# A short piece moved to the end of every value product, and the last 512 queries of the last head group cut in two

## The chip, the cores and the metric

The kernel runs on one NeuronCore of a Trainium2 chip. The metric is the device time of one execution in microseconds; the figure quoted is the median over the runs. TensorE (PE) does the matmuls, VectorE (DVE), ScalarE (ACT) and GpSimd (POOL) the elementwise work, and SyncE (SP) issues most transfers.

## What is computed

One input x (2048 rows, 512 columns, bf16) goes through two branches, and a gate per row mixes them. Branch A is attention with 32 heads of 16 and a sliding window of 256; branch B is a gated feed-forward layer of width 1376.

```python
def _A_ref(x, wqkv, wo):
    H = 32; Dh = D // H; W = 256
    q, k, v = qkv[0], qkv[1], qkv[2]
    scores = jnp.einsum("bhqd,bhkd->bhqk", q, k) * (Dh ** -0.5)
    mask = (idx[:, None] - idx[None, :] >= 0) & (idx[:, None] - idx[None, :] < W)
    scores = jnp.where(mask[None, None], scores, -1e9)
    p = _softmax(scores, axis=-1)
    o = jnp.einsum("bhqk,bhkd->bhqd", p, v)
    return o.transpose(...).reshape(B, S, D) @ wo

def _B_ref(x, w1, w3, w2):
    return (silu(x @ w1) * (x @ w3)) @ w2

g = sigmoid((x * gate_w).sum(-1, keepdims=True))
return g * _A_ref(x, A_wqkv, A_wo) + (1 - g) * _B_ref(x, B_w1, B_w3, B_w2)
```

## The kernel before

**Tiling of the attention.** The 32 heads form 4 groups c of 8 heads, and the queries form 4 tiles t of 512. Keys are taken in blocks of 64 (HK). A *piece* (j, q0, q1, col) is key block j against queries q0 to q1, written at column col of a score buffer. A block of 64 keys is seen by at most 320 queries (64 + 256), which is the widest piece; the narrowest has 64 queries. `bursts(c, t)` (L271) packs the pieces of a tile into *bursts* of up to 512 columns: 4 bursts for t = 0, 5 for each other tile, 76 over all groups.

**One burst** (`add_burst`, L663): for each piece 4 score matmuls on TensorE (L684; keys 32 x 128 are the stationary operand, which holds two heads' worth of 64 keys in its columns), into the tile `big`, of which there is one (4 banks of PSUM). ScalarE takes the exponential of it into a tile `e` (L692). Then triangles are masked, one at the near and one at the far edge of the window, where a piece has such an edge: on GpSimd with two instructions each (L708), or on VectorE (L702) for the far edges of bursts 2 and 3.

**One value product** (`add_pv`, L729): for each entry of `ranges(c, t)` (L267; here the whole tile of 512 queries) it collects all pieces of the tile's bursts, clipped to the range, into the list `work`, and issues 8 matmuls for each piece (L758). The eight use eight different parts of the array (two row groups of 64, four column groups of 32), and take 64 keys x 32 value columns as stationary operand; one of the value columns is 1 and gives the sum for the softmax. They accumulate in two banks of the pool `g`. VectorE then transposes both banks (L768), takes the reciprocal (L777), multiplies (L778) and transposes back into `OT` (L783). A tile of queries 512 and up has 12 pieces of 320, 192, 320, 192, 320, 128, 64, 320, 128, 64, 256 and 256 queries in this order; a tile of the first 512 has 9: 320, 192, 320, 128, 64, 320, 192, 320, 64.

**The rest on TensorE** is full matmuls of 128 x 512: projections of q and k (L313) and v (L360), the up products of the feed-forward layer (L454; a last slice of 96 columns at L504), the down products (L552), and the output projection (L582). The last 128 rows are done in another order (`add_last`, L601): output projection (L611) first, then the down product in column ranges of 256, 128 and 128 (L636), each with its own output transfer.

**The order of the work.** Every piece of work is an `Op` with a duration, dependencies and buffers, and a list scheduler (L872 to L1002) simulates the engines and writes each engine's order at build time; on the chip every engine then runs its list in order, with semaphores. Bursts, value products and projections have due times: `when(c, n) = T0 + PACE * (19 c + n)` (L807), with T0 = 12.5 and PACE = 2.62 (L803). On TensorE a burst that is due goes first; a value product goes behind a burst, or once it has been ready for 2.6 us, or when no burst is left (L953); an item with a due time that has passed goes ahead of the feed-forward work, which fills the rest. The durations in the scheduler for a value product are 0.14 us plus its columns over 2400 (L792), plus 0.1 if no burst is ahead of it.

`LAST` (L265) names the last tile of the last group, (3, 3). Its vector work gets a rank of its own (L796).

Of the kernel before, what the change touches and what calls it, by code (L numbers as in the profile page):

```python
# [16 lines left out]
HK = 64  # L17
# [5 lines left out]
def kernel(  # L23
# [68 lines left out]
    def hold(pool, key, n):  # L92

        refs[(pool, key)] = n
# [127 lines left out]
    def bank(key, dtype=F32, shape=(P, 512)):  # L222
        n = slot("g", key)
        g_tile[key] = ps.tile(list(shape), dtype, name=f"g{n}")
        return g_tile[key]
# [39 lines left out]
    LAST = (NDC - 1, NTC - 1)  # L265

    def ranges(c, t):  # L267

        return [(512 * t, 512 * t + 512)]

    def bursts(c, t):  # L271

        b, q = 8 * t, 512 * t
        if t == 0:
            r = [[(0, 0, 320), (5, 320, 512)], [(1, 64, 384), (6, 384, 512), (4, 448, 512)],
                 [(2, 128, 448), (4, 256, 448)], [(3, 192, 512), (7, 448, 512)]]
        else:
            r = [[(0, 0, 320), (-2, 0, 192)], [(1, 64, 384), (5, 320, 512)],
                 [(2, 128, 448), (6, 384, 512), (-4, 0, 64)],
                 [(3, 192, 512), (-3, 0, 128), (7, 448, 512)], [(-1, 0, 256), (4, 256, 512)]]  # L280
        out = []
        for ps_ in r:
            col, o = 0, []
            for j, q0, q1 in ps_:
                o.append((b + j, q + q0, q + q1, col))
                col += q1 - q0
            out.append(o)
        return out
# [4 lines left out]
    def add_proj(c, t0, t1, is_q):  # L293
# [8 lines left out]
        if first:  # L302
            hold("qk", (c, t), len(bursts(c, t)) + (len(bursts(c, t + 1)) if t + 1 < NTC else 0))
# [359 lines left out]
    def add_burst(c, t, n):  # L663


        key = (c, t, n)
        pieces = bursts(c, t)[n]
        w = sum(q1 - q0 for _, q0, q1, _ in pieces)
        hold("big", key, 1)
        hold("e", key, sum(any(q0 < b and q1 > a for _, q0, q1, _ in pieces) for a, b in ranges(c, t)))  # L670
        deps = []
        for j, q0, q1, _ in pieces:
# [56 lines left out]
    def add_pv(c, t, qa, qb):  # L729


        keys = [("p", c, qa, i) for i in range(2)]
        for k in keys:
            hold("g", k, 1)
        st = {}
        nq = qb - qa
        used, work = [], []
        for n, pieces in enumerate(bursts(c, t)):
            for j, q0, q1, col in pieces:
                a, b = max(q0, qa), min(q1, qb)  # L740
                if a < b:
                    work.append(((c, t, n), j, a, b, col + a - q0))
                    if (c, t, n) not in used:
                        used.append((c, t, n))
        rel = [("e", k) for k in used]

        def v_of(j, i, w):
            lo = i * HK
            if j % 2 == i:
                return Vn[lo:lo + HK, j // 2, i * VW + w * (DH + 1):i * VW + w * (DH + 1) + 32]  # L750
            return Vs[lo:lo + HK, j // 2, w * (DH + 1):w * (DH + 1) + 32]

        def pe():
            st["pv"] = pv = [bank(k) for k in keys]
            for n, (k, j, a, b, col) in enumerate(work):
                for i in range(2):
                    for u in range(4):
                        nc.tensor.matmul(pv[i][32 * u:32 * u + 32, a - qa:b - qa],  # L758
                                         lhsT=v_of(j, i, 4 * c + u),
                                         rhs=e_tile[k][i * HK:i * HK + HK, u, col:col + b - a],  # L760
                                         start=(n == 0), stop=(n == len(work) - 1),
                                         skip_group_check=True)

        def turn(i):
            def f(eng):
                if i == 0:
                    st["t1"] = xp.tile([P, 2, 512], F32, name="xs23")
                nc.vector.transpose(out=st["t1"][:, i, 0:nq], in_=st["pv"][i][:, 0:nq])  # L768
            return f

        nb = nq // 32

        def norm(eng):
            rden = sb.tile([P, 2, 16, 1], F32, name="rden")
            st["on"] = on = sb.tile([P, 16, 2, DH], BF16, name="on")
            v = st["t1"][:, :, 0:nq].rearrange("p i (b r) -> p i b r", r=32)
            nc.vector.reciprocal(out=rden[:, :, 0:nb, :], in_=v[:, :, :, DH:DH + 1])  # L777
            nc.vector.tensor_tensor(out=on[:, 0:nb].rearrange("p b i d -> p i b d"),  # L778
                                    in0=v[:, :, :, 0:DH],
                                    in1=rden[:, :, 0:nb, :].to_broadcast([P, 2, nb, DH]), op=ALU.mult)  # L780

        def back(eng):
            nc.vector.transpose(out=OT[:, c * S + qa:c * S + qb],  # L783
                                in_=st["on"][:, 0:nb].rearrange("p b i d -> p (b i d)"))

        deps = [o for k in used for o in e_mask[k]]
        js = [j for _, j, _, _, _ in work]
        deps += [V_op[m] for m in range(min(js) // 2, max(js) // 2 + 1)]
        deps += [Vs_op[x] for x in range(min(js) // 8, max(js) // 8 + 1)]
        hold("t1", ("t1", c, qa), 1)  # L790
        cols = sum(b - a for _, _, a, b, _ in work)
        a = Op("PE", 0.14 + cols / 2400.0, pe, deps, acq=[("g", k) for k in keys], rel=rel, kind="pv")  # L792
        b0 = Op("DVE", 0.1 + nq * 0.0012, turn(0), [a], rel=[("g", keys[0])],
                acq=[("t1", ("t1", c, qa))], rank=-0.6)
        b1 = Op("DVE", 0.1 + nq * 0.0012, turn(1), [a, b0], rel=[("g", keys[1])], rank=-0.6)
        rk = -0.3 if (c, t) == LAST else 0.6  # L796
        n1 = Op("DVE", 0.5 + nq * 0.0011, norm, [b0, b1], rank=rk)
        o = Op("DVE", 0.15 + nq * 0.0011, back, [n1] + (z_op if c else []), rel=[("t1", ("t1", c, qa))], rank=rk)
        for m in range(qa // P, qb // P):
            pv_out[(c, m)] = o  # L800
        return a

    T0, PACE, NWARM = 12.5, 2.62, 6  # L803
    SEQ = [(t, n) for t in range(NTC) for n in range(len(bursts(0, t)))]
    per_c = len(SEQ)

# [30 lines left out]
    for c in range(NDC):  # L837
        for n, (t, k) in enumerate(SEQ):
            a = add_burst(c, t, k)
            a.need = when(c, n)  # L840
        for t in range(NTC):
            for qa, qb in ranges(c, t):
                a = add_pv(c, t, qa, qb)
                a.need = when(c, SEQ.index((t, 0)) + 5) + 1.0
# [40 lines left out]
    def ready_time(o, eng):  # L885
        r = 0.0
        for d in o.deps:
            lat = 0.0 if d.eng == eng else LAT.get((d.eng, eng), 0.08)
            r = max(r, d.end + d.lag + lat)
        return r  # L890
# [22 lines left out]
    while len(order) < len(ops):  # L913
# [3 lines left out]
        for e, lst in ready.items():  # L917
            cands = []
            for o in lst:
                if o.kind == "ffn" and not o.cont and o.seq != ffn_next:  # L920
                    continue
                r = max(ready_time(o, e), free_at[e])
                ok = True
                want = {}
                for pool, key in o.acq:
# [4 lines left out]
                    r = max(r, sorted(slots[pool])[n - 1][0] + 0.08)  # L930
# [8 lines left out]
            t = max(min(r for r, _ in cands), free_at[e])  # L939
# [25 lines left out]
            r, o = min(now, key=pkey)  # L965
# [7 lines left out]
        t, e, o = best  # L973
# [72 lines left out]
```

The softmax here doesn't subtract the row's maximum and nothing guards it: scores larger than these inputs give would overflow.

## Time and profile before

| | |
|---|---|
| median of 4 runs | 231.54 us (231.15 to 232.07) |
| the profiled execution | 232.07 us, span 230.2 us |
| TensorE clock granted | 1.00 of full speed |
| TensorE busy | 221.9 us (96% of the span) |
| VectorE, ScalarE, GpSimd busy | 178.8, 177.5, 175.1 us |
| score matmuls (L684) | 720, of 188 to 305 ns each |
| value product matmuls (L758) | 1440, of 189 to 300 ns each |
| full matmuls of the up products (L454) | 302 recorded with 320 weight loads, 380 ns each |
| exponential of one burst (L692) | 1.88 us for 512 columns |
| one triangle instruction on GpSimd (L708) | 448 ns, 368 of them |

The span is the time from the first to the last instruction in the profile. In a timeline, a row has its start, its length (us), engine, line, operation, what it writes and reads, its shape, how often it is repeated, and in brackets the idle time of the engine ahead of it and what ended it. PE is TensorE's matmuls, PEld its weight loads, which run beside the matmuls. Matmuls are pipelined, so the length of one (380 ns) is longer than the distance between two starts.

### The profile page before, as it was taken

The page shows a single profiled execution, that of the slowest core. Times are in us where ns is not written, and L with a number is a line of the kernel's source. Part 1 is how long each engine was busy: PE and PEld are TensorE (multiplying, and loading weights), DVE is VectorE, ACT ScalarE, POOL GpSimd, SP SyncE. Part 2 cuts the span into 40 slices and gives each one's busy share as a digit, 9 for nine tenths or more (in the row PEclk, how much of TensorE's full clock was granted, in tenths as well). Part 3 has the DMA queues.
Part 4 walks back from the last instruction along what each step waited for, and adds up shares of the span by engine and source line. Part 5 has one row for each costly group of instructions (what it writes and reads, how often), then busy time and mean ns, then how long its engine had stood idle before and what let it go on. Part 6 is the DMA issues. An engine that isn't in the chain of part 4 may idle for free.

```text
span 230.2 us, 7237 instructions
## 1 busy us (share of the span) xinstructions
PE 221.9 (96%) x3026; PEld 102.2 (44%) x3060; DVE 178.8 (78%) x312; ACT 177.5 (77%) x148; POOL 175.1 (76%) x395
## 2 busy tenths in 40 slices
PE   7999999999999999999999999999999999999995
PEld 4543344535434443535453435443443445354544
DVE  1467789999999999768758593959987688876754
ACT  3579899889888899796989799987899877977030
POOL 8049888989988888888778887877888878778200
PEclk9999999999999999999999999999999999999999
DMA  6999999400200000000000000000000000220202
GB/s 185 219 274 341 156 277 362 106 0 4 48 3 3 3 0 0 4 3 4 0 3 0 3 3 0 3 3 4 1 3 0 3 4 25 81 83 0 94 3 93
DMA packets 19697, 13.81 MB, mean 60 GB/s; under 512 B 8656, under 2 KB 19376, under 8 KB 19664
## 3 DMA queue, kind: packets, MB, share of 16 engines
q1 hardware_dynamic: 18560, 11.93, 19.6%
q0 software_dynamic: 432, 1.25, 3.3%
q8 instruction: 24, 0.39, 0.7%
q10 hardware_dynamic: 672, 0.16, 0.3%
q14 instruction: 9, 0.07, 0.1%
HBM read 8.55 MB, written 2.10 MB: 46 GB/s over the span
## 4 chain that ended last, share of the span: by engine, by line
PE 84%; DVE 8%; DMA 3%; issue 2%; ACT 1%; SPq 1%; ACTq 0%
PE g L454 27%; PE g L552 16%; PE big L684 10%; PE g L313 10%; PE g L758 8%; PE g L582 6%; PE g L360 4%; DMA e<-in_A_wqkv_dram 3%; PE g L504 2%; DVE hT L462 2%; PE g L636 1%; DVE kt L328 1%; DVE Vn L370 1%; ACT e L692 1%; DVE h L435 1%
## 5 line engine op out<-in xcount | busy, mean ns | idle before, releaser
L708 POOL TENSOR_SCALAR_AFFINE_SELECT e<-e 64x256 bf16<-64x256 bf16 x368 | 164.7, 448 | 32.1 <-ACT e L692 11.4
L692 ACT ACTIVATE e<-big 128x2048 bf16<-128x2048 f32 (+1 forms) x76 | 141.0, 1855 | 29.3 <-PE big L684 27.7
L454 PE MATMUL g<-xT,w_sb 128*128 128x512 bf16 x302 | 76.3, 380 | 1.4 <-issue 1.0
L454 PEld LDWEIGHTS <-w_sb 128*128 128x128 bf16 x320 | 29.1, 98 | 35.2 <-issue 4.0
L552 PE MATMUL g<-w_sb,hT 128*128 128x512 bf16 (+1 forms) x159 | 38.9, 380 | 1.3 <-issue 1.3
L768 DVE STREAM_TRANSPOSE xs<-g 128x512 f32<-128x512 f32 x32 | 21.9, 701 | 17.8 <-PE g L758 17.8
L435 DVE SCALAR_TENSOR_TENSOR h<-tt,g 128x512 bf16<-128x512 bf16 (+1 forms) x44 | 29.8, 677 | 5.0 <-ACT tt L430 4.6
L462 DVE TENSOR_TENSOR hT<-h,g 128x512 bf16<-128x512 bf16 x40 | 26.9, 674 | 4.8 <-PE g L454 4.3
L684 PE MATMUL big<-qt,kt 32*128 32x64 bf16 (+3 forms) x720 | 30.0, 254 | 0.4 <-ACT e L692 0.2
L430 ACT ACTIVATE tt<-g 128x512 bf16<-128x512 f32 (+1 forms) x44 | 26.1, 594 | 1.2 <-PE g L454 0.5
L684 PEld LDWEIGHTS <-kt 32*128 32x128 bf16 x720 | 12.0, 92 | 32.8 <-issue 31.1
L552 PEld LDWEIGHTS <-hT 128*128 128x128 bf16 (+1 forms) x165 | 15.0, 98 | 17.8 <-issue 1.4
L328 DVE TENSOR_TENSOR kt<-g,maskEO 128x1024 bf16<-128x1024 f32 (+1 forms) x17 | 19.6, 1151 | 3.0 <-PE g L313 2.9
L758 PE MATMUL g<-e,Vs 64*32 64x64 bf16 (+3 forms) x720 | 20.0, 253 | 0.0
L758 PE MATMUL g<-e,Vn 64*32 64x64 bf16 (+3 forms) x720 | 19.9, 254 | 0.0
L313 PE MATMUL g<-xT,wq_sb 128*128 128x512 bf16 (+1 forms) x66 | 17.9, 368 | 0.4 <-issue 0.3
L313 PE MATMUL g<-xT,wk_sb 128*128 128x512 bf16 (+1 forms) x64 | 17.0, 375 | 0.4 <-issue 0.2
L758 PEld LDWEIGHTS <-Vn 64*32 64x32 bf16 x720 | 15.1, 91 | 3.4 <-issue 1.1
L360 PE MATMUL g<-e,xT 128*128 128x512 bf16 x61 | 15.5, 380 | 0.4 <-DMA e<-in_A_wqkv_dram 0.2
L758 PEld LDWEIGHTS <-Vs 64*32 64x32 bf16 x720 | 15.2, 91 | 0.2
L702 DVE TENSOR_TENSOR e<-e,keep 128x512 bf16<-128x512 bf16 (+1 forms) x32 | 14.0, 442 | 0.6 <-ACT e L692 0.5
L582 PE MATMUL g<-xs,OT 128*128 128x512 bf16 x59 | 14.1, 380 | 0.1
(61 smaller groups left out, 153.7 us busy)
## 6 DMA issues: line engine op xcount, KB each, us to landing
w_sb<-in_B_w_dram SPq DMA_DIRECT2D x2, 864.0 KB, 7.7
w_sb<-in_B_w_dram SPq DMA_DIRECT2D x1, 1280.0 KB, 10.0
out_dram<-ot SPq DMA_DIRECT2D x19, 64.0 KB, 1.6
Vs<-Vn POOLq DMA_DIRECT2D x8, 136.0 KB, 3.6
w_sb<-in_B_w_dram SPq DMA_DIRECT2D x2, 512.0 KB, 4.8
OT<-in_A_x_dram SPq DMA_DIRECT2D x1, 1024.0 KB, 10.8
out_dram<-ot SPq DMA_DIRECT2D x6, 128.0 KB, 1.8
xs<-in_A_x_dram SPq DMA_DIRECT2D x2, 256.0 KB, 3.2
```

The costliest lines, as they stand in the source:

```text
L313: nc.tensor.matmul(b[:, 0:n], lhsT=(wq_sb if is_q else wk_sb)[:, dc, c * P:(c + 1) * P], rhs=xT[:, dc, t0:t1], start=(dc == 0), stop=(dc = ...
L360: nc.tensor.matmul(b[:], lhsT=xT[:, c, m * P:(m + 1) * P], rhs=wv_sb[:, c, :], start=(c == 0), stop=(c == NDC - 1))
L430: nc.scalar.activation(out=tl["tt"][0:m, :], in_=g_tile[key][0:m, :], func=ACT.Tanh, scale=0.5)
L435: nc.vector.scalar_tensor_tensor(out=tl["h1"][0:m, :], in0=tl["tt"][0:m, :], scalar=1.0, in1=g_tile[key][0:m, :], op0=ALU.add, op1=ALU.mult)
L454: nc.tensor.matmul(b[:], lhsT=wsb[:, dc, f * P:(f + 1) * P], rhs=xT[:, dc, t * 512:(t + 1) * 512], start=(dc == 0), stop=(dc == NDC - 1))
L462: nc.vector.tensor_tensor(out=h_of(t)[:, f, :], in0=tl["h1"][:], in1=g_tile[ku][:], op=ALU.mult)
L552: nc.tensor.matmul(b[:], lhsT=h_tile[t][0:fs, f, (m % 4) * P:(m % 4 + 1) * P], rhs=w2_sb[0:fs, f, :], start=(f == 0), stop=(f == NFC - 1))
L582: nc.tensor.matmul(b[:, 0:n], lhsT=OT[:, c * S + m * P:c * S + (m + 1) * P], rhs=wo_t[c // 2][:, c % 2, n0:n1], start=(c == 0), stop=(c == ...
L684: nc.tensor.matmul(big[:, u, col:col + q1 - q0], lhsT=kt[32 * u:32 * u + 32, (j % 8) * P:(j % 8 + 1) * P], rhs=qt[32 * u:32 * u + 32, q0 - ...
L692: nc.scalar.activation(out=e[:, :, 0:w], in_=tl["big"][:, :, 0:w], func=ACT.Exp, scale=SCALE)
L708: nc.gpsimd.affine_select(out=tri, in_=tri, pattern=[[0, 4], [-1 if far else 1, HK]], compare_op=ALU.is_ge, fill=0.0, base=-1 if far else ...
L758: nc.tensor.matmul(pv[i][32 * u:32 * u + 32, a - qa:b - qa], lhsT=v_of(j, i, 4 * c + u), rhs=e_tile[k][i * HK:i * HK + HK, u, col:col + b ...
```

## The change

Three things change, and a number. `ranges` returns two ranges of 256 queries for the last tile of the last group, so that `add_pv` makes two value products there. `bursts` packs the pieces of that tile in another way, cut at 256 queries, into five bursts of 512 columns: 16 pieces in place of 12. In `add_pv`, where there is more than one piece, the first piece of exactly 64 queries is taken out of the list and put at its end, in every value product; the matmuls that open and close the accumulation are by position. T0 becomes 12.0.

For a tile of queries 512 and up the order of pieces becomes 320, 192, 320, 192, 320, 128, 320, 128, 64, 256, 256, 64; for the first 512: 320, 192, 320, 128, 320, 192, 320, 64, 64. Each half of the last tile has 256, 256, 192, 192, 128, 128, 64, 64 (second half: 256, 256, 192, 192, 128, 128, 64, 64 with other keys).

```diff
     def ranges(c, t):
 
-        return [(512 * t, 512 * t + 512)]
+        q = 512 * t
+        return [(q, q + 256), (q + 256, q + 512)] if (c, t) == LAST else [(q, q + 512)]
 
     def bursts(c, t):
...
+        elif (c, t) == LAST:
+            r = [[(0, 0, 256), (-1, 0, 256)], [(1, 64, 256), (-2, 0, 192), (2, 128, 256)],
+                 [(-3, 0, 128), (-4, 0, 64), (3, 192, 256), (4, 256, 512)],
+                 [(3, 256, 512), (5, 320, 512), (0, 256, 320)],
+                 [(2, 256, 448), (1, 256, 384), (6, 384, 512), (7, 448, 512)]]
         else:
             r = [[(0, 0, 320), (-2, 0, 192)], [(1, 64, 384), (5, 320, 512)],
...
                     if (c, t, n) not in used:
                         used.append((c, t, n))
+        short = [x for x in work if x[3] - x[2] == HK]
+        if len(work) > 1 and short:
+            work.remove(short[0])
+            work.append(short[0])
         rel = [("e", k) for k in used]
...
-    T0, PACE, NWARM = 12.5, 2.62, 6
+    T0, PACE, NWARM = 12.0, 2.62, 6
```

## The prediction

> **What bounds the kernel now.** I read the page first, then the timeline of TensorE, then the timeline around the end.
>
> ```profile
> span 230.2 us, 7237 instructions
> PE 221.9 (96%) x3026; PEld 102.2 (44%) x3060; DVE 178.8 (78%) x312; ACT 177.5 (77%) x148; POOL 175.1 (76%) x395
> PE 84%; DVE 8%; DMA 3%; issue 2%; ACT 1%; SPq 1%; ACTq 0%
> ```
>
> The page says that TensorE is the bound: 96% busy, and 84% of the chain that ended last. A busy share hides what a matmul really costs, so I took the distance from the first weight load of one kind of work to the first weight load of the next. Three kinds alternate on TensorE: full matmuls (128x512), score bursts (L684) and value products (L758). Next, the timeline of a value product of queries 512 and up, with the burst ahead of it and the full matmuls behind it.
>
> ```profile
> 202.60 0.40 PE L684 MATMUL big<-qt,kt 32*128 32x320 bf16 x8
> ...
> 202.93 0.10 PEld L758 LDWEIGHTS <-Vn 64*32 64x32 bf16 x4 [0.21 <-issue]
> ...
> 203.57 0.20 PE L758 MATMUL g<-e,Vn 64*32 64x64 bf16 x4
> ...
> 203.61 0.32 PE L758 MATMUL g<-e,Vn 64*32 64x320 bf16 x4
> ...
> 203.98 0.29 PE L758 MATMUL g<-e,Vs 64*32 64x256 bf16 x4
> ...
> 204.21 0.76 PEld L454 LDWEIGHTS <-w_sb 128*128 128x128 bf16 x5
> ```
>
> The product takes 204.21 - 202.93 = 1.28 us for 12 pieces of 8 matmuls. The eight run side by side, so its pieces stream 2560 columns. A column costs 0.42 ns: the 16 matmuls of 512 columns at 211.80 take 3.62 us with a last one of 0.38, so (3.62 - 0.38) / 15 = 0.216 us each. That makes 2560 columns 1.08 us, and 0.20 us is lost. The same for a product of the first 512 queries, whose last piece has 64 columns and not 256:
>
> ```profile
> 129.41 0.32 PE L758 MATMUL g<-e,Vn 64*32 64x320 bf16 x4
> ...
> 130.22 0.21 PE L758 MATMUL g<-e,Vn 64*32 64x64 bf16 x4
> 130.36 0.11 PEld L552 LDWEIGHTS <-hT 128*128 128x128 bf16 x2
> ```
>
> It takes 0.95 to 0.96 us for 9 pieces with 1920 columns, that is 0.81 us, and loses 0.15. After the first groups of its last piece the next kind starts 0.15 us later; with 256 columns at the end it is 0.23 us. All 16 products of the trace repeat these two figures within 0.01 us (12 of 1.28, 4 of 0.96).
>
> TensorE's stretches of full matmuls add up too: 10 matmuls between two bursts take 2.27 us, which is 2.16 + 0.11 for the change of kind, and a burst takes 0.33 (202.60 to 202.93). From 8.34 us, when the weights of the value projection have landed, to the last matmul I find one stretch that is longer than this count, by 0.28 us:
>
> ```profile
> 32.04 1.88 ACT L692 ACTIVATE e<-big 128x2048 bf16<-128x2048 f32 x1 [0.19 <-PE big L684]
> ...
> 33.68 0.09 PEld L684 LDWEIGHTS <-kt 32*128 32x128 bf16 x1 [0.42 <-issue]
> ...
> 33.96 0.40 PE L684 MATMUL big<-qt,kt 32*128 32x256 bf16 x8 [0.21 <-ACT e L692]
> ```
>
> Here a burst had its weights at 33.68 but the one score buffer was still read by the exponential, which ended at 33.92. So the time is the sum of TensorE's work, plus 8.3 us ahead of it and 2.7 us behind it. The gaps of 0.16 us that the page puts down to issue are mostly matmuls missing from the records: the weight loads there are complete.
>
> **The change, part by part.** (1) *The short piece goes last* in the 11 whole products of queries 512 and up (12 less the split one). Same 96 matmuls and loads each. What it can save is the loss at the end: 0.20 against 0.15 us, since the product would end as those of the first 512 queries do. The start times say why: behind the sequence of a 128 and a 64 piece the loads no longer run ahead, the last two pieces of 256 start their eight matmuls spread over about 0.06 us, and the 256 columns stream after that. I take 0.045 us each, 11 x 0.045 = -0.50. Bounds: nothing is gained if the product is set by its number of matmuls (12 x 8 x 13.3 ns = 1.28 fits as well), and a last piece that is issued late loses 0.03 each; at best 0.06 each. So -0.66 to +0.33. In the four products of the first 512 queries a 64 piece goes behind another 64 piece: 4 x 0.01 = -0.04.
>
> (2) *The last product is split* into two halves of 256 queries. Each has 8 pieces (256, 256, 192, 192, 128, 128, 64, 64) with 1280 columns: 0.54 us and, as it ends on a 64, 0.15 lost: 0.69. Two are 1.38 in place of 1.28: **+0.10**. By the count of matmuls it would be 2 x 64 x 13.3 ns = 1.71, +0.43; that is the upper end, and +0.05 the lower (both halves losing 0.12). One more product may stand alone between full matmuls: +0.11 or nothing, I take +0.05, as the bursts of the last queries are still running when the first half is ready.
>
> The Trainium skill speaks against more and smaller matmuls: the page TensorEngine Tiling (Array Packing), section Instruction Overhead, gives every matmul about 60 cycles whatever its width. The rows differ: eight 64 column matmuls cost 0.04 us (203.57 to 203.61), 5 ns each, since they lie on eight tiles. By the page the 32 added matmuls would be 32 x 25 ns at its 2.4 GHz, an estimate of +0.8 us, and the whole change about +0.4 instead of what follows.
>
> (3) *Five bursts of the last queries are cut otherwise.* Each still has 512 columns (0.33 us), but 16 matmuls and loads more in all. A 64 piece between others streams 0.03 us and may wait for the next load. Bounds 0 (a burst of 2 and of 3 pieces both take 0.33) and +0.13 (two such places, each with the 92 ns of a load at L684 less 27). I take +0.05.
>
> (4) *Masks and VectorE.* GpSimd's triangles stay 12, but the last burst has 4 in place of 2. VectorE gets a second chain of transposes, reciprocal, product and transpose, of half the width; this is at most the 3.2 us of a whole one. All of it costs nothing if TensorE has other work meanwhile. The timeline of the end:
>
> ```profile
> 210.59 0.40 PE L684 MATMUL big<-qt,kt 32*128 32x256 bf16 x8
> ...
> 211.12 1.88 ACT L692 ACTIVATE e<-big 128x2048 bf16<-128x2048 f32 x1 [0.74 <-POOL e L708]
> ...
> 213.07 1.80 POOL L708 TENSOR_SCALAR_AFFINE_SELECT e<-e 64x256 bf16<-64x256 bf16 x4 [0.53 <-ACT e L692]
> ...
> 216.21 0.32 PE L758 MATMUL g<-e,Vn 64*32 64x320 bf16 x4
> ...
> 220.03 0.71 DVE L783 STREAM_TRANSPOSE OT<-on 128x512 bf16<-128x512 bf16 x1
> ...
> 221.40 1.03 PE L611 MATMUL g<-xs,OT 128*128 128x512 bf16 x4
> ```
>
> The chain behind the product ends at 220.74, 0.66 us before TensorE asks for it. With four triangles (3.6 us) and a last burst 0.5 us earlier the second half is ready near 216.2; even at 217.5 it ends at 218.2, and a chain of 3.2 us at 221.4. Work that does not need it lasts longer: from the last burst TensorE has 16.5 + 0.5 us, of which the projections of the last 256 queries and the last down products (0.86 + 0.86 + 2.45) depend on it, so the rest reaches to about 223. Slack 1.8 us. Without that cover each us of lateness would be a us of time. Transfers: no DMA is added, and output rows leave as before.
>
> (5) *T0 from 12.5 to 12.0* moves the due times of all bursts, products and projections 0.5 us ahead of the feed-forward work. It adds no work, and TensorE is full from 8.34 on, so there is nothing to win but the 0.28 us at 33.68. It can lose where a burst comes before its buffer is free, or where VectorE is full:
>
> ```profile
> 40.00:60.00 20.00, 19.49 (x327) 9.33 (x332) 19.61 (x38) 16.94 (x14) 17.90 (x37) 1.00 0.18 44
> ```
>
> In this row of the stretches VectorE (the third pair) is busy 19.61 of 20 us, and evacuates most of what TensorE writes. I take 0, with -0.28 to +0.6.
>
> **Sum:** -0.50 - 0.04 + 0.10 + 0.05 + 0.05 + 0 = -0.34 us. The profiled execution took 232.07 with a span of 230.2, so its span would be 229.9. It is 0.53 above the median of 231.54; on the median the forecast is **231.2 us**.
>
> **Rivals.** *A, clearly faster.* The ends add: -0.66 - 0.04 + 0.05 + 0 + 0 - 0.28 = -0.93 at the very most; with most of these, 230.75. For it: the one stall is due to the order, which changes. Against: nearly all must come true, as no other idle time exists.
>
> *B, the moved piece does nothing,* because a product is set by its number of matmuls. Then 0 + 0.43 + 0.11 + 0.05 = +0.59: 232.1. For it: 1.28 / 96 and 0.96 / 72 are both 13.3 ns. Against: starts inside a product follow the widths (0.13 us behind 320 columns, 0.04 behind 64), not the count.
>
> *C, slower:* the earlier bursts meet the full VectorE between 40 and 64 us. A burst's share of VectorE work there (a mask of 0.4, a fifth of a 3.2 us chain and of two evacuations of 1.8 together) is 1.2 to 1.4 us; if it runs ahead of the evacuations that free TensorE's buffers, TensorE stands still for about that long: -0.34 + 1.3 = +1.0, 232.5. It decides from a wait of 1.03 us on, below that the gain covers it. For it: the chain of waits runs through VectorE there without a gap. Against: eight gate reductions of about 0.8 us stand in the same stretch and can wait.
>
> **How the numbers follow.** A measurement of this kernel can tell about 0.3% (0.7 us) from no change: below 230.85 is faster, above 232.23 slower. Forecast 0.45 and B 0.06 lie between; A 0.27; C 0.22. So faster 0.27, same 0.51, slower 0.22. The range goes to A and C: 230.6 to 232.6; the forecast's own is 230.9 to 231.6.
>
> **What would show it.** Right: products of queries 512 and up last 1.23 us from first load to the next kind's load, halves 0.69, stretches of full matmuls keep 0.11 + 0.216 each, and the last matmul ends near 227.1. Products still at 1.28 and halves at 0.85 show B. A stretch of full matmuls or a burst more than 0.1 us over its count, with VectorE ahead of it, shows C; the same with the exponential ahead shows that the stall at 33.68 moved or grew. Wrong altogether would be an idle TensorE ahead of the last output projections.

## The result, and the profile after

The changed kernel takes 232.10 us (median of 47 runs), the kernel before 231.58 us (72 runs). The ratio is **1.0023, with a 95% interval of 1.0018 to 1.0028**: slower by half a microsecond, where a third of one less was forecast. The change is below the bound of 0.3% of the prediction, yet well outside the interval, and its sign is wrong. The measured 232.10 lies inside the wide range that the prediction's rivals had set (230.6 to 232.6) and outside the forecast's own (230.9 to 231.6).

The page of the changed kernel, the lines that answer to those shown of before:

```profile
span 230.2 us, 7347 instructions
PE 221.5 (96%) x3074; PEld 102.9 (45%) x3108; DVE 175.9 (76%) x310; ACT 180.2 (78%) x155; POOL 174.0 (76%) x395
PE 88%; DVE 4%; issue 3%; DMA 2%; ACT 1%; SPq 1%; DVEq 0%; ACTq 0%
```

The two spans are equal to 0.1 us, so the pages alone hide the loss. The profiled executions (231.87 and 232.07 us) lie on opposite sides of their medians, and the reason is at the start: the weights of the value projection had landed for a first matmul at 7.56 us after the change, at 8.34 before. I therefore measure from the first matmul of the value projection to the end of the last matmul, where TensorE has no pause of more than 0.06 us but the named ones: 8.34 to 227.45 = **219.11 us before, 7.56 to 227.38 = 219.82 after: +0.71**. This distance, always of the one profiled execution, is given for experiments below.

A whole product of queries 512 and up in the changed kernel, in the timeline (start, length, engine, line; lines are 6 to 10 higher than before, the value matmul is L768):

```profile
142.48 0.10 PEld L768 LDWEIGHTS <-Vn 64*32 64x32 bf16 x4
...
143.32 0.20 PE L768 MATMUL g<-e,Vn 64*32 64x64 bf16 x4
143.34 0.28 PE L768 MATMUL g<-e,Vs 64*32 64x256 bf16 x4
...
143.56 0.22 PE L768 MATMUL g<-e,Vn 64*32 64x64 bf16 x4
143.59 0.21 PE L768 MATMUL g<-e,Vs 64*32 64x64 bf16 x4
143.74 0.10 PEld L319 LDWEIGHTS <-wk_sb 128*128 128x128 bf16 x1
```

It takes 143.74 - 142.48 = 1.26 us (1.257 in the trace's nanoseconds), not 1.28 and not the forecast 1.23. The product does end 0.15 us behind the start of its second row group's last matmuls (143.59), as said. But its last eight matmuls still start over 60 ns (143.56 and on), not over the 35 ns of a product of the first 512 queries before the change. In nanoseconds from the first load, the last matmul starts at 1139, where before it started at 1081; it then streams 192 columns fewer (81 ns), which leaves a gain of 23 ns.

The first half of the split product:

```profile
211.01 0.26 PEld L690 LDWEIGHTS <-kt 32*128 32x128 bf16 x16 [0.43 <-issue]
...
211.35 0.10 PEld L588 LDWEIGHTS <-OT 128*128 128x128 bf16 x1
...
211.67 0.10 PEld L768 LDWEIGHTS <-Vn 64*32 64x32 bf16 x4 [0.23 <-issue]
...
212.21 0.27 PE L768 MATMUL g<-e,Vn 64*32 64x64 bf16 x8
...
212.44 0.55 PEld L588 LDWEIGHTS <-OT 128*128 128x128 bf16 x4
```

It takes 0.77 us (212.44 - 211.67), so two halves are 1.54 in place of 1.28. And between the burst (0.34 us with its 16 loads) and the product there is a stretch of one single full matmul (211.35 to 211.67, 0.32 us = 0.216 + 0.11). That is a change of kind which did not exist before.

There are more of those. Counted over the whole trace, full matmuls stand in 81 stretches, against 77 before. One is the half's, another is a single matmul ahead of a product at 79.64, and two stand behind a group of the tiled up products (L510) at 29.86 and here:

```profile
157.01 0.55 PEld L510 LDWEIGHTS <-w_sb 128*32 128x32 bf16 x16 [0.42 <-issue]
157.99 0.11 PEld L460 LDWEIGHTS <-w_sb 128*128 128x128 bf16 x2 [0.42 <-issue]
158.53 0.25 PEld L690 LDWEIGHTS <-kt 32*128 32x128 bf16 x12 [0.42 <-issue]
```

Two full matmuls between tiled ones and a burst take 0.54 us: 0.43 of work, 0.11 for the change. Last come the waits. The 0.28 us at 33.7 us is gone, and another has come near it:

```profile
33.34 1.23 DVE L334 TENSOR_TENSOR kt<-g,maskEO 128x1024 bf16<-128x1024 f32 x1
33.37 0.76 PEld L460 LDWEIGHTS <-w_sb 128*128 128x128 bf16 x5 [0.21 <-issue]
33.37 1.04 PE L460 MATMUL g<-xT,w_sb 128*128 128x512 bf16 x4
...
34.62 1.02 PE L460 MATMUL g<-xT,w_sb 128*128 128x512 bf16 x4 [0.21 <-DVE kt L334]
```

TensorE's up product waits until VectorE has read the keys out of a `g` buffer, which it finishes at 34.57: 0.37 us over the count for that stretch. And one product, at 90.26 us, stands still in the middle:

```profile
91.12 0.28 PE L768 MATMUL g<-e,Vs 64*32 64x256 bf16 x4
91.13 0.31 PEld L768 LDWEIGHTS <-Vn 64*32 64x32 bf16 x8
91.33 0.30 PE L768 MATMUL g<-e,Vn 64*32 64x256 bf16 x8
```

Its piece of 256 has started for one row group and waits 0.2 us for the other. GpSimd masks that burst meanwhile. The third of its five triangle instructions in this row ends at 91.28, and TensorE goes on 0.05 us later, at 91.33:

```profile
89.93 2.28 POOL L714 TENSOR_SCALAR_AFFINE_SELECT e<-e 64x256 bf16<-64x256 bf16 x5
```

The ledger, from the trace:

| part | us |
|---|---|
| ten products at 1.257, three at 0.948 | -0.25 |
| two halves in place of a whole | +0.26 |
| four more changes of kind, 0.11 each | +0.44 |
| wait at 33 us: 0.37 in place of 0.28 | +0.09 |
| product at 90.26 (1.423) and at 79.96 (1.005) against 1.280 and 0.958 | +0.19 |
| sum, against 0.71 measured in these two executions | +0.73 |

The product at 79.96 loses its 0.05 us at its start: one row group starts at once, the other at 80.03, which is 0.06 behind the end of a triangle instruction (79.97). This fits the same wait for a mask.

### The profile page after: what moved, and what is told of

It is laid out like the page before. It is cut to its first block, busy times and chain, and to the rows that moved or that the text cites. A ratio compares the mean times of both kernels' runs of the same rounds, so it can differ in the third digit from the quotient of the medians.

```text
span 230.2 us, 7347 instructions
## 1 busy us (share of the span) xinstructions
PE 221.5 (96%) x3074; PEld 102.9 (45%) x3108; DVE 175.9 (76%) x310; ACT 180.2 (78%) x155; POOL 174.0 (76%) x395
## 4 chain that ended last, share of the span: by engine, by line
PE 88%; DVE 4%; issue 3%; DMA 2%; ACT 1%; SPq 1%; DVEq 0%; ACTq 0%
PE g L460 29%; PE g L558 16%; PE g L319 11%; PE big L690 10%; PE g L768 8%; PE g L366 6%; PE g L588 6%; DMA e<-in_A_wqkv_dram 2%; PE g L510 1%; PE g L642 1%; DVE h L441 1%; DVE hT L518 1%; DVE xs L778 1%; DVE kt L334 1%; ACT tt L436 1%
## 5 line engine op out<-in xcount | busy, mean ns | idle before, releaser
L460 PEld LDWEIGHTS <-w_sb 128*128 128x128 bf16 x320 | 28.5, 98 | 35.7 <-issue 5.7
L778 DVE STREAM_TRANSPOSE xs<-g 128x512 f32<-128x512 f32 (+1 forms) x34 | 21.9, 669 | 16.9 <-PE g L768 16.7
L690 PE MATMUL big<-qt,kt 32*128 32x64 bf16 (+4 forms) x736 | 30.1, 252 | 0.3
L768 PE MATMUL g<-e,Vs 64*32 64x320 bf16 (+4 forms) x736 | 20.2, 251 | 0.0
L768 PE MATMUL g<-e,Vn 64*32 64x320 bf16 (+4 forms) x736 | 20.0, 252 | 0.0
L768 PEld LDWEIGHTS <-Vn 64*32 64x32 bf16 x736 | 15.6, 91 | 3.3 <-issue 1.9
L319 PE MATMUL g<-xT,wq_sb 128*128 128x512 bf16 (+1 forms) x66 | 16.7, 367 | 0.3 <-issue 0.3
L768 PEld LDWEIGHTS <-Vs 64*32 64x32 bf16 x736 | 15.6, 92 | 0.3
L366 PE MATMUL g<-e,xT 128*128 128x512 bf16 x61 | 14.8, 379 | 0.6 <-DMA e<-in_A_wqkv_dram 0.2
```

The lines of the kernel that those rows point to most:

```text
L319: nc.tensor.matmul(b[:, 0:n], lhsT=(wq_sb if is_q else wk_sb)[:, dc, c * P:(c + 1) * P], rhs=xT[:, dc, t0:t1], start=(dc == 0), stop=(dc = ...
L366: nc.tensor.matmul(b[:], lhsT=xT[:, c, m * P:(m + 1) * P], rhs=wv_sb[:, c, :], start=(c == 0), stop=(c == NDC - 1))
L460: nc.tensor.matmul(b[:], lhsT=wsb[:, dc, f * P:(f + 1) * P], rhs=xT[:, dc, t * 512:(t + 1) * 512], start=(dc == 0), stop=(dc == NDC - 1))
L690: nc.tensor.matmul(big[:, u, col:col + q1 - q0], lhsT=kt[32 * u:32 * u + 32, (j % 8) * P:(j % 8 + 1) * P], rhs=qt[32 * u:32 * u + 32, q0 - ...
L768: nc.tensor.matmul(pv[i][32 * u:32 * u + 32, a - qa:b - qa], lhsT=v_of(j, i, 4 * c + u), rhs=e_tile[k][i * HK:i * HK + HK, u, col:col + b ...
```

## The experiments

My theory after the result: the change is a sum of three independent parts, of which the moved piece gains, the split loses, and T0 = 12.0 loses because the scheduler makes another order of work out of it. Rivals stand with each run. All ratios are against the kernel before, run on the same chip.

**The moved piece alone.**

```diff
+        short = [x for x in work if x[3] - x[2] == HK]
+        if len(work) > 1 and short:
+            work.remove(short[0])
+            work.append(short[0])
```

> Before, with the short piece moved to the end and nothing else (T0 12.5, last tile whole). The order of work on TensorE is that of before, 77 stretches of full matmuls. Theory (three parts that add up: a small gain from the moved piece, a loss from the split, a loss from the order that T0 = 12.0 makes): products of queries 512 and up 1.257 us as in the changed kernel, 948 ns for the first 512, so 12 x -0.022 + 4 x -0.010 = -0.30 us, ratio 0.9987. Rival (the moved piece itself is what costs, through VectorE's or the buffers' timing): no gain or a loss, ratio 1.000 or more.

Ratio 0.9986 (0.9978 to 0.9995), 231.26 us; twelve products of 1.256 to 1.258 and four of 0.947 to 0.948; 77 stretches; distance 218.87, that is -0.24. The theory holds, the rival falls: this part is a gain.

**The split alone.**

```diff
-        return [(512 * t, 512 * t + 512)]
+        return [(q, q + 256), (q + 256, q + 512)] if (c, t) == LAST else [(q, q + 512)]
...
+        elif (c, t) == LAST:
+            r = [...]
```

> Before, with the last tile of the last group split (ranges and bursts) and nothing else (T0 12.5, pieces in their old order). TensorE's order has 78 stretches of full matmuls in place of 77. Theory: two halves of 0.77 us in place of one product of 1.28 (+0.26) and one more change of kind (+0.11): +0.37 us, ratio 1.0016. Rival of the prediction on record (halves of 0.69 us): +0.10 to +0.21, ratio 1.0004 to 1.0009.

Ratio 1.0018 (1.0009 to 1.0027). The halves take 0.768 and 0.751 us, there are 78 stretches, and the distance is 219.46, +0.35, which is 0.24 + 0.11. The prediction's 0.69 for a half is out. The second half takes 0.768 in the changed kernel, so the moved piece costs 0.017 there.

**T0 = 12.0 alone.**

```diff
-    T0, PACE, NWARM = 12.5, 2.62, 6
+    T0, PACE, NWARM = 12.0, 2.62, 6
```

> Before, with T0 = 12.0 and nothing else. TensorE's order has 80 stretches of full matmuls in place of 77. Theory: 3 x 0.11 for the changes of kind, a stall of 0.37 us near 33 us in place of one of 0.28, one product that waits 0.17 us for a mask near 90 us and one that starts badly behind a single full matmul (0.05): +0.6 us, ratio 1.0027. Rival (T0 only shifts work that is hidden, the split accounts for the whole loss): ratio 1.000.

Ratio 1.0019 (1.0009 to 1.0030); distance 219.60, +0.48. 80 stretches, the wait of 0.37 at 33.3 us, and the product at 90 us at 1.360, 0.08 late and not the expected 0.17; the one behind the single full matmul is not late (0.957). These name 0.33 + 0.09 + 0.08 = 0.50. The rival falls. The three parts alone are -0.0014 + 0.0018 + 0.0019 = +0.0023, the whole change is +0.0023; as distances -0.24 + 0.35 + 0.48 = +0.59, against 0.71. So the parts do not quite add up in the traces. The two products that wait for masks name the rest: in the changed kernel they are 0.17 and 0.06 us over the 1.257 and 0.948 of the others, with T0 alone 0.08 and nothing. With the 64 piece at the end, TensorE reaches the piece of 256 that waits for a mask at 0.86 us into the product and not at 0.91, and GpSimd is no earlier.

**The changed kernel with T0 back at 12.5.**

```diff
-    T0, PACE, NWARM = 12.0, 2.62, 6
+    T0, PACE, NWARM = 12.5, 2.62, 6
```

> The changed kernel with T0 back at 12.5, so the split and the moved piece stay. TensorE's order has 78 stretches of full matmuls in place of the changed kernel's 81 and of 77 before. Theory (three parts that add up): moved piece alone 0.9986, split alone 1.0018, so 1.0004, that is +0.1 us, clearly below the changed kernel's 1.0023; no wait of 0.17 us in a product and the stall near 33 us back to 0.28. Rival (the parts act on each other, T0 = 12.0 suits the split): 1.0023 or more.

Ratio 1.0000 (0.9986 to 1.0014), lower than the changed kernel's 1.0018 to 1.0028. So T0 is worth about 0.2% with the split in place too, and the rival falls. The stall near 33 us is 0.28 again, and no product waits. The distance of its profiled execution alone would not show this: it is 219.73, +0.62, of which 0.57 is a wait near 42 us that comes and goes between executions (see the last section).

**What a product's time consists of: the widest piece last.** For the next two, `work` is put in the order given.

```diff
+        line = []
+        for w in {12: [320, 192, 320, 64, 320, 128, 192, 64, 256, 128, 256, 320], 9: [...]}[len(work)]:
+            line.append(next(x for x in work if x[3] - x[2] == w and x not in line))
+        work = line
```

> Before, with the pieces of each product in another order: 320, 192, 320, 64, 320, 128, 192, 64, 256, 128, 256, 320 (and 320, 192, 320, 64, 320, 128, 192, 64, 320 for the first 512 queries), so that every narrow piece is followed by a wide one and the widest is last. Theory (a product loses time when the weight loads stop running ahead, which happens behind a 128 and a 64 piece next to each other; a narrow end is not what matters): 1.235 us in place of 1.28 and 0.955 as before, 12 x -0.045 = -0.54 us, ratio 0.9977. Rival (the width of the last piece is what is saved): 1.28 us or more, ratio 1.000 or more.

Ratio 1.0015 (1.0005 to 1.0026): my theory failed. The products take 1.284, and those of the first 512 queries 1.010 in place of 0.957. The end of one, in this kernel's timeline (value matmul L763):

```profile
143.28 0.40 PE L763 MATMUL g<-e,Vs 64*32 64x256 bf16 x8
143.31 0.11 PEld L763 LDWEIGHTS <-Vn 64*32 64x32 bf16 x4
...
143.39 0.32 PE L763 MATMUL g<-e,Vn 64*32 64x320 bf16 x4
143.64 0.33 PEld L454 LDWEIGHTS <-w_sb 128*128 128x128 bf16 x3 [0.22 <-issue]
```

In nanoseconds the trace shows why. From the sixth piece on, two behind the first 64, the weight loads come one by one, 8.3 ns apart, where those of the first pieces come 3 to 4 ns apart; from the ninth on the matmuls do so too. My reading is that the early narrow pieces have used up what was issued ahead: the last piece is issued late (its last matmul starts at 1.06 us, before at 1.08 with 256 columns left), and then its 320 columns must still stream. By this both matter: narrow pieces should come late, and the last should be narrow. What the products measured adds 12 x 0.004 + 4 x 0.053 = +0.26 us, and a wait of 0.38 us at 42 us (see the last section) made this execution longer.

**Narrow pieces late and apart.**

> Before, with each product's pieces in the order 320, 192, 320, 192, 320, 128, 320, 64, 256, 128, 256, 64 (first 512 queries: 320, 192, 320, 128, 320, 192, 320, 64, 64), so narrow at the end as with the moved piece, but the other narrow ones late and apart. Theory (issue of load and matmul pairs at 8.3 ns limits a product once narrow pieces have used up the lead, so narrow pieces must be late and apart, and the last one narrow): 1.231 us, 12 x -0.048 - 4 x 0.01 = -0.62 us, ratio 0.9973. Rival (the moved piece has already all of it): 1.257 us, ratio 0.9986.

Ratio 0.9980 (0.9971 to 0.9989); the products take 1.257 and 0.947, as with the moved piece (1.257 and 0.948). The interval of the ratio takes in both forecasts; the products decide, and by them the rival holds: the moved piece has all there is in this, since the last eight start over 60 ns here as well.

**Sixteen pieces, one product.**

```diff
-        return [(q, q + 256), (q + 256, q + 512)] if (c, t) == LAST else [(q, q + 512)]
+        return [(q, q + 512)]
```

> Before, with the five bursts of the last tile cut as in the change (16 pieces) but one whole value product for it, pieces in their order, T0 12.5, 77 stretches. What makes two halves cost 0.26 us more than a whole one? Theory (the 32 added pairs of load and matmul, which are issued 8.3 ns apart): the last product takes 1.28 + 0.27 = 1.55 us, ratio 1.0012. Rival (what a product loses at its start and end, 0.2 us, is paid twice): 1.28 to 1.32 us, ratio 1.000.

Neither number: the product takes 1.400 us. The run with the split alone has the same pieces in the same order as two halves, 0.768 + 0.751 = 1.52. So of its +0.24 the added pairs make 0.12, and the second start and end 1.52 - 1.40 = 0.12. The kernel as a whole has the ratio 1.0034 (1.0023 to 1.0045), and the timeline shows the missing part:

```profile
221.32 0.71 DVE L789 STREAM_TRANSPOSE OT<-on 128x512 bf16<-128x512 bf16 x1
222.09 0.10 PEld L617 LDWEIGHTS <-OT 128*128 128x128 bf16 x1 [1.07 <-DVE OT L789]
222.09 0.39 PE L617 MATMUL g<-xs,OT 128*128 128x512 bf16 x1 [0.57 <-DVE OT L789]
```

GpSimd's four triangles behind the last burst end at 215.93, and the scheduler's order has 33 full matmuls between that burst and the product, where before it has 24. So the whole product is late (217.34 us), its chain ends at 222.03, and the last projection of `OT` waits for it, about 0.7 us over the count. This is the cover of the prediction's step (4), seen gone. In the changed kernel the second half begins later still (218.81), but from its first load to the end of its chain takes 2.9 us, where the whole product takes 4.7, and nothing waits:

```profile
221.26 0.45 DVE L793 STREAM_TRANSPOSE OT<-on 128x256 bf16<-128x256 bf16 x1
...
222.84 0.74 PEld L617 LDWEIGHTS <-OT 128*128 128x128 bf16 x4
```

**The halves in another order.**

```diff
+        if len(work) == 8:
+            for w in (256, 256, 128, 192, 64, 192, 128, 64): ...
```

> The changed kernel with T0 = 12.5 and, in the two halves alone, the pieces in the order 256, 256, 128, 192, 64, 192, 128, 64, so that narrow ones do not stand together. Theory (64 pairs of load and matmul are issued at 8.3 ns each, and the halves have too many for their columns): a half stays at 0.74 to 0.77 us. Rival (it is the row of narrow pieces at the end): 0.69 us, as the prediction on record had it.

The halves take 0.741 us each, in place of 0.768: the theory holds, and the narrow pieces at the end cost 0.027, no more. The kernel took 231.55 us in a single run.

**Other values of T0,** each with the short piece last (expected 0.9986 without T0's part).

```diff
-    T0, PACE, NWARM = 12.5, 2.62, 6
+    T0, PACE, NWARM = 13.25, 2.62, 6
```

> Before, with the short piece last (as measured alone: 0.9986) and T0 = 13.25, which gives an order with 75 stretches of full matmuls and 4 of the tiled up products, three changes of kind fewer than before (T0 = 12.0 gives three more). Theory (T0 acts through the number of changes of kind, 0.11 us each, and single stalls of 0.1 to 0.4 us): 0.9986 less 3 x 0.11 / 231.5 = 0.9972, give or take one stall, so 0.996 to 0.999. Rival (a due time away from 12.5 costs, whatever the count): above 1.000.

Ratio 1.0090 (1.0075 to 1.0106): my count failed as a forecast. It has three changes fewer and is 2 us slower, all by waits. Two products stand still inside and take 2.13 and 2.11 us in place of 0.95 and 1.26; a wait of 0.95 near 30 us is for VectorE's transposes, and one of 0.29 at 157.7 for the exponential. The first of the products ran from 78.30 to the load at 80.43; the timeline of GpSimd and the end of the product:

```profile
75.59 7.77 POOL L708 TENSOR_SCALAR_AFFINE_SELECT e<-e 64x256 bf16<-64x256 bf16 x15
...
80.43 0.98 PEld L552 LDWEIGHTS <-hT 128*128 128x128 bf16 x6
```

GpSimd has no pause from 75.59 on, about 0.5 us for each instruction, and in the trace the rest of the product's third last piece and its two last ones start at 79.31, 79.78 and 80.26, one such instruction apart and each 0.05 us behind the end of one: the product was begun before its masks. The second product's other row group starts 0.88 us late, just as VectorE has read the feed-forward branch out of a `g` buffer, which fits a wait for its second bank; the trace does not name it.

> Before, with the short piece last and T0 = 11.75, earlier than the change's 12.0. TensorE's order: 76 stretches of full matmuls and 4 of the tiled up products (77 and 5 with 12.5; 80 and 5 with 12.0 alone). Theory (T0 is no lever of its own; each value gives another order, and what it costs are that order's changes of kind and its waits): 0.9986 - 2 x 0.11 / 231.5 = 0.9977 if no new wait, higher with waits that the trace names. Rival (an earlier T0 costs as such): more than T0 = 12.0 costs, so above 0.9986 + 0.0019 = 1.0005.

Ratio 1.0025 (1.0009 to 1.0041) with 76 stretches. That is the loss that the rival forecast, but the trace has waits that are enough for all of it: one product takes 1.33 in place of 0.95, 0.24 us are lost at 33.2, and 0.58 at 160.9, where VectorE's reading of the keys (L328) is late:

```profile
161.10 1.23 DVE L328 TENSOR_TENSOR kt<-g,maskEO 128x1024 bf16<-128x1024 f32 x1
...
162.38 0.81 PE L454 MATMUL g<-xT,w_sb 128*128 128x512 bf16 x3 [0.41 <-DVE kt L328]
```

> Before, with the short piece last and T0 = 12.6; 77 stretches of full matmuls and 5 tiled, as with 12.5. Theory: no more changes of kind, so 0.9986, and other waits of up to 0.4 us. Rival (a later T0 helps as such): below 0.998.

Ratio 0.9982 (0.9968 to 0.9997): 77 stretches and no new wait. The theory's 0.9986 fits; the interval also reaches below the rival's 0.998, so this run does not exclude it.

> Before, with the short piece last and T0 = 12.25, half of the change's step; 78 stretches and 5 tiled. Theory (by the order): 0.9986 + 0.11 / 231.5 = 0.9991, and other waits of up to 0.4 us. Rival (by the value): half of the loss of T0 = 12.0, so 0.9986 + 0.0010 = 0.9996; these two can be told apart only by the trace.

Ratio 0.9987 (0.9969 to 1.0004): 78 stretches, waits of 0.14 and 0.12 us, one product 0.04 late, and the 0.28 near 33 us gone. From 12.25 to 12.6 T0 makes no difference that these runs can tell; 12.0 loses by three more changes of kind and by waits, 11.75 and 13.25, which have fewer changes than before, by waits alone; the traces name them. Whether an earlier T0 costs as such, besides, these few values do not settle: both orders made with a T0 of 12.0 or less lose.

The moved piece with T0 at 12.5 or 12.6 beats both kernels (0.9986 and 0.9982); at 12.25 its interval still reaches 1.0004. The lowest ratio measured, 0.9980 with the other order of pieces, is not to be told from these.

## Why the prediction was wrong

**Step (5), T0 at nothing, is the one that failed.** "It adds no work" is false: an order of work has a number of changes between full, tiled, score and value matmuls, and each further stretch of full matmuls costs TensorE 0.11 us in these traces, the figure that the prediction itself had read. T0 = 12.0 makes three more of them, and moves and makes waits. Alone it is +0.0019, about +0.44 us, in the bounds given for it (-0.28 to +0.6) but far from the value taken. Between the forecast of -0.34 and the measured +0.52 lie 0.86 us; by the ratios of the runs alone T0 makes half of it, and the sizes of steps (1) and (2) make about 0.2 each. With T0 at 12.5 and those two as they are, the ratio was 1.0000. The 0.28 us that the prediction found at 33.68 were also not the only pause before: the stretch of full matmuls at 79.91 is 0.06 over its count.

**Step (1), the moved piece,** was right in sign and too large: 0.022 us for each product, not 0.045. The product ends on 64 columns as said, but the last eight matmuls start over 60 ns and not 35, as the last eight of 256 columns did, so the end did not become that of a product of the first 512 queries. Alone it measured -0.32 us by the ratio, where -0.54 stood for 11 products and the four small ones.

**Step (2), the split,** was too small: a half takes 0.77, not 0.69, so +0.26 and not +0.10. The 0.15 us that a product of nine pieces loses does not carry over to one of eight pieces that has two thirds of the columns and one narrow piece more. The change of kind ahead of the first half came in full, 0.11 for the 0.05 taken. The bounds held (+0.05 to +0.43). As for the rule from the Trainium skill's page TensorEngine Tiling (Array Packing), section Instruction Overhead: 32 added matmuls cost 0.12 us in one product, 4 ns each, and 0.26 us in two halves, 8 ns each with a second start and end included, against the 25 ns that were worked out from the page as an estimate. The measurement decides. The prediction's own 0.04 us for eight 64 column matmuls was a misreading (203.57 and 203.61 are starts of different row groups): from the first start of that piece to the first of the next it is 0.028.

**Step (3)** was nearly nothing: a burst with 16 loads takes 0.34 us, in place of 0.33. **Step (4)** was right: nothing waited for VectorE or GpSimd at the end, where the chain ended at 221.71 and TensorE asked for it at 222.84, 1.1 us of slack for the 1.8 said. The run with one product and four triangles shows the price without that cover, about 0.7 us.

**The rivals.** A did not come: the wait at 33 us went, but another took its place. B's sum, 232.1, is what was measured, by luck: its mechanism is not what happened, since the moved piece does gain. C named the right mechanism, TensorE standing still for VectorE, in the wrong place (33 us, not 40 to 64) and at 0.37 us, below the 1.03 from which it was to decide.

## What to carry to other kernels

Where one engine is full and its work is of several kinds, count the changes of kind in the order that a scheduler will make, before and after: a constant that moves due times is not free because it adds no instruction. The count alone is no forecast: T0 = 13.25 and 11.75 have fewer changes than before and were slower. So look where each item's inputs are ready only in the scheduler's model, since those waits came out larger than the changes (2 us net for 0.75 on T0). Undo the parts of a bundled change one by one: here a part worth -0.14% lay hidden under two of +0.18% and +0.19%.

## What the runs showed of the hardware that was not expected

TensorE's small matmuls come in two regimes: pairs of load and matmul start 3 to 4 ns apart as long as they were issued ahead, and 8.3 ns apart from the point on where narrow pieces have used up the lead; with eight pairs a piece, one of 64 columns then takes 66 ns (the eighth piece of the product of 16) in place of 28 (the seventh of a product before).

The first matmul of the value projection starts between 7.20 and 8.34 us in the profiled executions of the fourteen kernels. In twelve of them TensorE stands idle before it, waiting for its weights to land; in the split alone and at T0 = 11.75 it comes straight from the projections of q. This alone is 1.1 us of spread between executions, twice the effect studied.

A wait near 42 us, between a burst and the projection of keys behind it, comes and goes between executions whose order is the same there: of the eight profiles with T0 = 12.5 three have none (before, the moved piece alone, the split alone) and five have 0.18 to 0.57 us. What it waits for, the records don't show.
